# Seven products in another order, and three sums of tokens made later: attention, mixture of experts and a gated layer on one core

## The chip, the cores and the metric

The kernel runs on one core of a Trainium2 chip. The metric is the time of one execution on the device in microseconds (us); the median of several runs counts. Less is better.

## The reference

Three layers follow each other; all inputs of the kernel are 64-bit floats, and the result is a 32-bit float.

```python
attn = softmax(causal(q @ k.T / 8)) @ v            # 4 x 12 heads, 448 tokens, 64 wide
x = attn as [1792, 768]
x = moe(x)      # 8 experts, each takes its 224 best tokens: relu(x @ w1[e]) @ w2[e]
gate = 1 / (1 + exp(-(x @ w_gate)))                # [768, 1536]
val = x @ w_val                                    # [768, 1536]
out = (gate * val) @ w_out                         # [1536, 768]
```

The change touches the last layer alone.

## The kernel before, in words

Attention runs first, then the routing of the tokens, then the eight experts one after the other, and then the gated layer in two halves of 896 tokens: `moe2a` and `moe2b`. A half consists of two blocks of 448 tokens, `bb` = 0 and 1. The hidden width of 1536 is cut into 12 slices `f` of 128. For two slices at a time, both halves make gate and value, multiply them to h, and add h times w_out to `acc` (`out_stage`: 84 matmuls of 384 columns for seven token tiles; it takes h of the even slice first, then h of the odd slice, for each tile). A 32-bit product is made of three matmuls: every operand is split into a high part (a copy by ScalarE, "hi") and the rest (a subtraction, "lo"), and hi·hi, hi·lo and lo·hi are added in PSUM. `h_parts` (lines 933 and 934) does this for h, on ScalarE and then VectorE.

**Weights.** The first half converts the 64-bit weights as they are first used (`conv_split`, lines 83 to 94): ScalarE makes the low word's share (line 83) and a square (line 85), VectorE works through lines 87, 88, 89 and 92, ScalarE makes hi (line 93) and VectorE lo (line 94). Each slice comes as two half tiles. The converted weights are also written to DRAM (`wsc`).

**The first half, `moe2a`**, makes plain products: 72 matmuls of 448 columns for each slice.

**The second half, `moe2b`**, treats two slices times two halves of the width of 768 times two token blocks as a 2 x 2 block product and makes it with seven products of sums in place of eight. The sums of weights are made on GpSimd in `combine`, a pair of slices ahead of their use. The sums of tokens are made once, also on GpSimd: three in `stage` (lines 974 to 976, after four loads of x on SyncE's queue, line 972), one in `stage_parts` (line 984); `stage` is called in `moe2a` ahead of slice 6. The results of the seven products are added up by VectorE (lines 1013 and 1022 to 1026); `done(o, add, e, bb)` finishes h of slice e (0 or 1 of the pair) and block bb: line 1013 the last sum, then for the gate (n = 0) a sigmoid on ScalarE, and for the value (n = 1) line 1019 the product with the gate, and `h_parts`. Then `out_stage` begins with tiles 4, 5 and 6, which need block 1 alone, and goes on to tile 3 and to block 0.

**What sets the order.** TensorE takes its matmuls in the order in which the code writes them. For the other engines and the DMA queues a scheduler picks an order when the kernel is built, from its own estimate and from priorities (`tc.high_priority`); on the chip each engine then works through its fixed list and waits at the first instruction that isn't ready.

Of the kernel before, what the change touches and what calls it, by code (L numbers as in the profile page):

```python
# [7 lines left out]
F32 = mybir.dt.float32  # L8
# [5 lines left out]
OP = mybir.AluOpType  # L14
# [10 lines left out]
HMIN = 3.4332275390625e-05  # L25
# [5 lines left out]
def body(ctx: ExitStack, tc: tile.TileContext, q, k, v, moe_w_gate, moe_w1, moe_w2,  # L31
         w_gate2, w_val2, w_out2, out):
    nc = tc.nc
# [11 lines left out]
    x2_d = dram.tile([2, 128, KD, 448], F32, name="x2_d")  # L45
# [8 lines left out]
    NF = F2 // 128  # L54
# [6 lines left out]
    g64, v64, o64 = (w.bitcast(U32) for w in (w_gate2, w_val2, w_out2))  # L61
    cv = ctx.enter_context(tc.tile_pool(name="cv", bufs=2))

    xst = []

    def conv_half(kind, f, n, hn, ln):
        cs = cv.tile([128, HC, 2], U32, name="cs", bufs=2)
# [11 lines left out]
    def conv_split(cs, hn, ln):  # L79


        hw, lw = cs[:, :, 1], cs[:, :, 0]
        nc.scalar.activation(lw, lw, AF.Copy, scale=2.0 ** -29)
        sq = cv.tile([128, HC], F32, name="sq", bufs=1)
        nc.scalar.activation(sq, hw.bitcast(F32), AF.Square)
        a = cv.tile([128, HC], U32, name="ca")
        nc.vector.tensor_scalar(a, hw, 3, 0x3FFFFFF8, op0=OP.logical_shift_left, op1=OP.bitwise_and)
        nc.vector.scalar_tensor_tensor(a, hw, 0xC0000000, a, op0=OP.bitwise_and, op1=OP.bitwise_or)
        nc.vector.tensor_tensor(a, a, lw, op=OP.add)  # L89

        w_ = a.bitcast(F32)
        nc.vector.scalar_tensor_tensor(w_, sq, HMIN * HMIN, w_, op0=OP.is_ge, op1=OP.mult)  # L92
        nc.scalar.activation(hn, w_, AF.Copy)
        nc.vector.tensor_tensor(ln, w_, hn.bitcast(F32), op=OP.subtract)  # L94
        return w_
# [58 lines left out]
    V = nc.vector  # L154
# [319 lines left out]
    HO = 5000  # L474
# [201 lines left out]
    def wt(dt=F32R):  # L676
        return mp.tile([128, CH], dt, name="w", bufs=WB)
# [53 lines left out]
    def combine(n, f):  # L731
        raw = cv.tile([128, HC, 2], U32, name="cs", bufs=2).rearrange("p f t -> p (f t)").bitcast(F32)
        for e in range(2):
            nc.sync.dma_start(raw[:, e * 768:(e + 1) * 768], wsc[wsc_n["gv", f + e]][:, 0, n * 768:(n + 1) * 768])
        a11, a12, a21, a22 = (raw[:, i * 384:(i + 1) * 384] for i in range(4))
        tl = [(wt(), wt()) for _ in range(2)]
        got = {}

        def parts(m, src, t, s_):
            hi, lo = (x[:, s_ * 384:(s_ + 1) * 384] for x in tl[t])  # L740
            nc.scalar.activation(hi, src, AF.Copy)  # L741
            nc.gpsimd.tensor_tensor(lo, src, hi.bitcast(F32), op=OP.subtract)  # L742
            got[m] = (hi, lo)

        TT = nc.gpsimd.tensor_tensor
        parts(1, a11, 0, 0)
        parts(4, a22, 0, 1)
        TT(a22, a21, a22, op=OP.add)
        parts(5, a22, 0, 2)
        TT(a21, a11, a21, op=OP.subtract)  # L750
        TT(a11, a22, a11, op=OP.subtract)
        parts(6, a11, 0, 3)
        TT(a22, a12, a11, op=OP.subtract)
        parts(7, a21, 1, 0)
        parts(3, a22, 1, 1)
        parts(2, a12, 1, 2)
        return got

    def load_half(kind, a, c, n, raw):
# [12 lines left out]
    def use(key):  # L772
        while key not in W:
            load_chunk()
        return W[key]
# [123 lines left out]
    def xq():  # L899
        return mp.tile([128, 3, 448], F32R, name="xq", bufs=8)  # L900
# [31 lines left out]
    def h_parts(hx, bb, o):  # L932
        nc.scalar.activation(hx[:, 0, bb], o, AF.Copy)
        nc.vector.tensor_tensor(hx[:, 1, bb], o, hx[:, 0, bb].bitcast(F32), op=OP.subtract)  # L934

    def moe2a():
        idxf = m2.tile([128, NT], I32, name="idxf", bufs=1)
        acc = m2.tile([128, NT, DM], F32, name="acc", bufs=1)
        gs = []
        for f in range(NF):  # L940
            if f == NF // 2:
                stage()
            wh, wl = use(("gv", 0, f))
            wv = [(wh[:, n * 768 + d * 128:n * 768 + (d + 1) * 128], wl[:, n * 768 + d * 128:n * 768 + (d + 1) * 128])
                  for n in range(2) for d in range(KD)]
            hx = mp.tile([128, 2, 2, 448], F32R, name="hx", bufs=3)
            for bb in range(2):
                x2h, x2l = X2[bb]
                xx = [(x2h[d // 3][:, d % 3, :], x2l[d // 3][:, d % 3, :]) for d in range(KD)]
                pg = ps.tile([128, 512], F32, name="g", bufs=7)  # L950
                prods(pg[:, :448], list(zip(wv[:KD], xx)))
                gv = m2.tile([128, 448], F32, name="gv", bufs=2)
                nc.scalar.activation(gv, pg[:, :448], AF.Sigmoid)
                pv = ps.tile([128, 512], F32, name="g", bufs=7)
                prods(pv[:, :448], list(zip(wv[KD:], xx)))
                nc.vector.tensor_tensor(pv[:, :448], pv[:, :448], gv, op=OP.mult)
                h_parts(hx, bb, pv[:, :448])
            gs.append(hx)
            if f % 2 == 1:
                out_stage(0, f - 1, gs, acc, idxf, range(NT))  # L960
                gs = []
# [4 lines left out]
    def xs(dt=F32R):  # L966
        return m2.tile([128, 3, 448], dt, name="xs", bufs=6)

    def stage():
        b11, t2, t1, t3, b22, b21 = (xs(F32) for _ in range(6))  # L970
        for t, kh, bb in ((b11, 0, 0), (t3, 0, 1), (b22, 1, 1), (b21, 1, 0)):
            nc.sync.dma_start(t, x2_d[bb][:, 3 * kh:3 * kh + 3])
        TT = nc.gpsimd.tensor_tensor
        TT(t1, t3, b11, op=OP.subtract)
        TT(t2, b22, t1, op=OP.subtract)
        TT(t3, b22, t3, op=OP.subtract)
        XR.update({1: b11, 6: t2, 5: t1, 7: t3, 3: b22, 2: b21})
# [3 lines left out]
    def stage_parts():  # L981
        t4 = cv.tile([128, HC, 2], U32, name="cs", bufs=2).rearrange("p f t -> p (f t)").bitcast(F32)
        XR[4] = t4[:, :3 * 448].rearrange("p (c t) -> p c t", c=3)
        nc.gpsimd.tensor_tensor(XR[4], XR[2], XR[6], op=OP.subtract)
        for m in (1, 6, 5, 7, 3, 2, 4):
            hi, lo = xq() if m == 1 else xs(), xq()
            nc.scalar.activation(hi, XR[m], AF.Copy)
            nc.vector.tensor_tensor(lo, XR[m], hi.bitcast(F32), op=OP.subtract)
            XS[m] = (hi, lo)

    def moe2b():
        idxf = m2.tile([128, NT], I32, name="idxf", bufs=1)
        acc = m2.tile([128, NT, DM], F32, name="acc", bufs=1)
        stage_parts()
        m1, u2, u3 = (cv.tile([128, HC], dt, name=nm, bufs=b).bitcast(F32)[:, :448]
                      for dt, nm, b in ((U32, "ca", 2), (U32, "ca", 2), (F32, "sq", 1)))
        of = o1.rearrange("p t c -> p (t c)").bitcast(F32)
        sgs = [m2.tile([128, 448], F32, name="gv", bufs=2) for _ in range(2)] + [of[:, :448], of[:, 448:]]
        for f in range(0, NF, 2):
            hx = [mp.tile([128, 2, 2, 448], F32R, name="hx", bufs=3) for _ in range(2)]  # L1000
            for n in range(2):
                qd = use((f"s{n}", 1, f))

                def prod(m):
                    o = ps.tile([128, 512], F32, name="g", bufs=7)[:, :448]
                    prods(o, [tuple((t[0][sl], t[1][sl]) for t, sl in ((qd[m], (slice(None), slice(d * 128, (d + 1) * 128))),
                                                                      (XS[m], (slice(None), d))))
                              for d in range(3)])
                    return o

                def done(o, add, e, bb):

                    V.tensor_tensor(o, o, add, op=OP.add)
                    sg = sgs[2 * e + bb]
                    if n == 0:
                        nc.scalar.activation(sg, o, AF.Sigmoid)
                    else:
                        with tc.high_priority(HO):
                            V.tensor_tensor(o, o, sg, op=OP.mult)
                            h_parts(hx[e], bb, o)  # L1020

                nc.scalar.activation(m1, prod(1), AF.Copy)
                V.tensor_tensor(u2, prod(6), m1, op=OP.add)
                p5 = prod(5)
                V.tensor_tensor(u3, prod(7), u2, op=OP.add)
                V.tensor_tensor(u2, p5, u2, op=OP.add)
                done(p5, u3, 1, 1)
                done(prod(3), u2, 0, 1)
                done(prod(2), m1, 0, 0)
                done(prod(4), u3, 1, 0)  # L1030
            out_stage(1, f, hx, acc, idxf, (4, 5, 6, 3, 0, 1, 2))

    ctx.enter_context(tc.manual_schedule(engines={mybir.EngineType.PE}))
# [40 lines left out]
```

## Time and profile before

| | |
|---|---|
| median of 3 runs | 1130.82 us (1128.95 to 1131.06) |
| the profiled execution | 1130.21 us |
| its span, first to last instruction | 1128.4 us |
| TensorE, matmuls | 1076.9 us busy (95%) |
| VectorE | 699.1 us (62%) |
| ScalarE | 439.5 us (39%) |
| GpSimd | 270.2 us (24%) |
| mean granted clock of TensorE | 0.979 |

In the span, attention reaches to about 245 us, the routing to 283, the experts to 602, the first half of the gated layer to 875 and the second half to the end. TensorE is busy nearly throughout, so what counts is where it stands still. The lines below are of three kinds: a line of the waits says who waited for whom, for how long in total, how often, and how long at most; a line of the timeline gives start, duration, engine, line of the code, operation, tile written and tiles read, and in brackets the idle time ahead of it with what ended it; a line of the windows gives a stretch and its length, the busy time of PE (TensorE), its weight loads, DVE (VectorE), ACT (ScalarE) and POOL (GpSimd), then the granted clock, the share of the DMA engines and their rate.

### The profile page before, as it was taken

To read this page: it belongs to the slowest core of one execution; us is meant where nothing else is said; L and a number is where in the kernel's file an instruction comes from. 1 tells how busy PE (TensorE), PEld (TensorE's weight loads), DVE (VectorE), ACT (ScalarE), POOL (GpSimd) and SP (SyncE) were. 2 spreads that over 40 slices of the span, in tenths; PEclk is the share of its full clock that TensorE was granted. 3 is DMA by queue.
4 is the path that set the end of the run, shared out by engine and by line. 5 is a ranking of instruction groups with operands and counts; after the bars stand their busy time and mean duration, and the time that the engine had idled before them with its cause. 6 is when DMAs were issued, how large, how long until landed. Compare 5 with 4: busy or idle time off the path is not lost.

```text
span 1128.4 us, 19849 instructions
## 1 busy us (share of the span) xinstructions
PE 1076.9 (95%) x7401; PEld 1020.8 (90%) x7401; DVE 699.1 (62%) x1980; ACT 439.5 (39%) x846; POOL 270.2 (24%) x371
## 2 busy tenths in 40 slices
PE   6999999982999999999999899999999999999997
PEld 6999999971899999999999799999999899899897
DVE  5777777766555556442557989878736515435535
ACT  4767677730111111123454465543414442322310
POOL 7333333300000000000000300000125746546522
PEclk9999999995999999999999899999999999999999
DMA  8556565525687667786747676655311521220212
GB/s 173 121 124 170 117 166 122 145 82 97 228 197 193 128 178 193 165 210 181 226 154 226 240 250 229 236 169 191 93 81 56 183 87 54 97 99 29 85 57 98
DMA packets 156991, 167.26 MB, mean 148 GB/s; under 512 B 74576, under 2 KB 140128, under 8 KB 156640
## 3 DMA queue, kind: packets, MB, share of 16 engines
q1 hardware_dynamic: 153472, 154.74, 46.1%
q0 software_dynamic: 2496, 11.04, 5.3%
q8 instruction: 58, 0.95, 0.4%
q10 hardware_dynamic: 928, 0.23, 0.1%
q14 instruction: 37, 0.30, 0.1%
HBM read 122.32 MB, written 32.64 MB: 137 GB/s over the span
## 4 chain that ended last, share of the span: by engine, by line
PE 90%; DVE 5%; issue 1%; DMA 1%; POOL 1%; ACT 1%; POOLq 0%; SPq 0%; ACTq 0%; DVEq 0%
PE g L778 67%; PE o L348 8%; PE w L328 4%; PE s L295 3%; PE s L296 2%; PE r L503 2%; PE w L257 1%; PE g L820 1%; DMA x_d<-x2f 1%; PE w L386 1%; PE w L369 1%; DVE ca L89 1%; DVE w L94 1%; DVE ca L92 0%; DVE hx L934 0%
## 5 line engine op out<-in xcount | busy, mean ns | idle before, releaser
L778 PE MATMUL g<-xq,w 128*128 128x448 f32 x1188 | 282.1, 367 | 0.0
L778 PEld LDWEIGHTS g<-xq,w 128*128 128x128 f32 x1188 | 222.7, 188 | 21.4
L778 PE MATMUL g<-w,hx 128*128 128x384 f32 x1008 | 181.6, 338 | 7.9 <-DVE hx L934 5.8
L778 PEld LDWEIGHTS g<-w,hx 128*128 128x128 f32 x1008 | 176.4, 190 | 12.0 <-DVE hx L934 8.3
L778 PE MATMUL g<-xx,w 128*128 128x224 f32 x768 | 151.4, 339 | 0.0
L778 PE MATMUL g<-hx,w 128*128 128x224 f32 x864 | 151.2, 331 | 0.0
L778 PEld LDWEIGHTS g<-hx,w 128*128 128x128 f32 x864 | 137.6, 191 | 2.5 <-issue 1.0
L778 PEld LDWEIGHTS g<-xx,w 128*128 128x128 f32 x768 | 134.9, 191 | 2.2 <-issue 0.2
L778 PE MATMUL g<-xs,w 128*128 128x448 f32 x432 | 124.7, 365 | 0.0
L742 POOL TENSOR_TENSOR w<-cs,w 128x384 fp32r<-128x384 f32 x84 | 84.2, 1024 | 121.4 <-ACT w L741 121.3
L348 PE MATMUL o<-vt,pt 112*112 112x65 f32 x960 | 106.3, 258 | 0.0
L348 PEld LDWEIGHTS o<-vt,pt 112*112 112x112 f32 x960 | 101.9, 178 | 0.0
L923 DVE TENSOR_TENSOR acc<-g,acc 128x384 f32<-128x384 f32 x140 | 75.3, 554 | 33.3 <-PE g L778 32.3
L298 DVE CUSTOM_DVE_ANT_0 sm<-s,mask 112x112 f32<-112x112 f32 (+1 forms) x192 | 78.4, 445 | 23.0 <-PE s L296 23.0
L306 ACT ACTIVATE sm<-sm,mn 112x112 f32<-112x112 f32 (+1 forms) x192 | 90.3, 522 | 5.1 <-DVE mn L298 5.1
L778 PEld LDWEIGHTS g<-xs,w 128*128 128x128 f32 x432 | 81.1, 188 | 6.2
L803 POOL DMA_INDIRECT xg<-x_d,ids x16 | 15.4, 962 | 296.3 <-DVE ids L622 105.4
L268 POOL CAST st<-hi 64x448 fp32r<-64x448 f32 x96 | 53.3, 556 | 133.4 <-ACT hi L263 122.8
L741 ACT ACTIVATE w<-cs 128x384 fp32r<-128x384 f32 x84 | 40.0, 518 | 92.4 <-PE g L778 48.7
L295 PE MATMUL s<-st,st 128*112 128x112 f32 (+1 forms) x192 | 62.2, 339 | 3.0 <-POOL st L268 2.6
L328 PE MATMUL w<-ident,sm 112*112 112x112 f32 x480 | 62.7, 261 | 0.1
L296 PE MATMUL s<-lo,qz 128*112 128x112 f32 (+1 forms) x192 | 56.5, 309 | 0.0
(214 smaller groups left out, 1450.0 us busy)
## 6 DMA issues: line engine op xcount, KB each, us to landing
w<-in_moe_w_dram SPq DMA_DIRECT2D x96, 384.0 KB, 6.6
raw<-in_moe_w_dram SPq DMA_DIRECT2D x32, 384.0 KB, 4.6
cs<-in_moe_w_gate_dram SPq DMA_DIRECT2D x12, 768.0 KB, 4.2
cs<-in_moe_w_val_dram SPq DMA_DIRECT2D x12, 768.0 KB
wsc<-ca SPq DMA_DIRECT2D x24, 384.0 KB, 4.7
cs<-in_moe_w_out_dram SPq DMA_DIRECT2D x12, 768.0 KB, 4.2
wsc<-w SPq DMA_DIRECT2D x12, 768.0 KB, 4.0
cs<-wsc SPq DMA_DIRECT2D x24, 384.0 KB, 3.1
```

Of the source, the lines that this page charges most:

```text
L268: nc.gpsimd.tensor_copy(st[r, h], hi[r].bitcast(F32))
L295: nc.tensor.matmul(ss[j], qq[:, j, qs], kh[:, j, :w], start=True, stop=False)
L296: nc.tensor.matmul(ss[j], QZ[u % NZ][:, j, qs], kl[:, :w], start=False, stop=True)
L298: nc.vector.tensor_tensor_reduce(sm[:, j, :w], ss[j], mask[:, S - w:], op0=OP.add, op1=OP.min, scale=1.0, scalar=3.0e38, accum_out=mn[:, j ...
L306: nc.scalar.activation(sm[:, j, :w], sm[:, j, :w], AF.Exp, bias=mn[:, j:j + 1], scale=-1.0)
L328: nc.tensor.transpose(w[:P, n, :], sm[:, j, c * P:(c + 1) * P], ident[:P, :P])
L348: nc.tensor.matmul(o[:, n, j, :], pt[:, j * (i + 1) + c, :], vt[:, j, c, :], start=c == 0, stop=c == i)
L503: nc.tensor.matmul(c[:, :J], oha[:, tt_, :], cmps[2 * tt_ // T][:, tt_ % (T // 2), :J], start=tt_ == 0, stop=tt_ == T - 1)
L741: nc.scalar.activation(hi, src, AF.Copy)
L742: nc.gpsimd.tensor_tensor(lo, src, hi.bitcast(F32), op=OP.subtract)
L778: nc.tensor.matmul(o, a, b, start=first, stop=last_)
L923: nc.vector.tensor_tensor(ac, po[:, :384], ac, op=OP.add)
```

## The change

Four edits, all in the gated layer:

- `moe2b` makes its seven products in the order 1, 2, 6, 5, 3, 7, 4; before, it was 1, 6, 5, 7, 3, 2, 4. h of slice 0, block 0 is finished first, then slice 0, block 1, then slice 1, block 1 (which needs products 7 and 5), then slice 1, block 0.
- `combine` makes the sums of weights in an order to fit, and places the parts of products 1, 2, 5, 6 in its first tile and 3, 7, 4 in its second. The number of copies, subtractions and sums stays.
- `stage` is called ahead of the products of slice 11 in place of slice 6, and its four loads wait for line 92 of the last half tile of slice 11's weights.
- `h_parts` in `moe2a` gets a high priority.

```diff
-    xst = []
+    xst, cvi = [], []
...
-        nc.vector.scalar_tensor_tensor(w_, sq, HMIN * HMIN, w_, op0=OP.is_ge, op1=OP.mult)
+        cvi.append(nc.vector.scalar_tensor_tensor(w_, sq, HMIN * HMIN, w_, op0=OP.is_ge, op1=OP.mult).ins)
...
...
         parts(1, a11, 0, 0)
-        parts(4, a22, 0, 1)
-        TT(a22, a21, a22, op=OP.add)
-        parts(5, a22, 0, 2)
-        TT(a21, a11, a21, op=OP.subtract)
-        TT(a11, a22, a11, op=OP.subtract)
-        parts(6, a11, 0, 3)
-        TT(a22, a12, a11, op=OP.subtract)
-        parts(7, a21, 1, 0)
-        parts(3, a22, 1, 1)
-        parts(2, a12, 1, 2)
+        parts(2, a12, 0, 1)
+        TT(a11, a11, a21, op=OP.subtract)
+        TT(a21, a21, a22, op=OP.add)
+        parts(5, a21, 0, 2)
+        TT(a21, a22, a11, op=OP.subtract)
+        parts(6, a21, 0, 3)
+        TT(a12, a12, a21, op=OP.subtract)
+        parts(3, a12, 1, 0)
+        parts(7, a11, 1, 1)
+        parts(4, a22, 1, 2)
...
         for f in range(NF):
-            if f == NF // 2:
+            wh, wl = use(("gv", 0, f))
+            if f == NF - 1:
                 stage()
-            wh, wl = use(("gv", 0, f))
...
-                h_parts(hx, bb, pv[:, :448])
+                with tc.high_priority(HO):
+                    h_parts(hx, bb, pv[:, :448])
...
         for t, kh, bb in ((b11, 0, 0), (t3, 0, 1), (b22, 1, 1), (b21, 1, 0)):
-            nc.sync.dma_start(t, x2_d[bb][:, 3 * kh:3 * kh + 3])
+            d_ = nc.sync.dma_start(t, x2_d[bb][:, 3 * kh:3 * kh + 3])
+            tc.add_manual_dep(d_.ins, cvi[-1].name, mybir.DependencyInfo(mybir.DependencyClass.Sync,
+                                                                         mybir.DependencyReason.DATA),
+                              reason="the weights first")
...
                 nc.scalar.activation(m1, prod(1), AF.Copy)
+                done(prod(2), m1, 0, 0)
                 V.tensor_tensor(u2, prod(6), m1, op=OP.add)
                 p5 = prod(5)
-                V.tensor_tensor(u3, prod(7), u2, op=OP.add)
-                V.tensor_tensor(u2, p5, u2, op=OP.add)
-                done(p5, u3, 1, 1)
-                done(prod(3), u2, 0, 1)
-                done(prod(2), m1, 0, 0)
-                done(prod(4), u3, 1, 0)
+                V.tensor_tensor(u3, p5, u2, op=OP.add)
+                done(prod(3), u3, 0, 1)
+                V.tensor_tensor(u2, prod(7), u2, op=OP.add)
+                done(p5, u2, 1, 1)
+                done(prod(4), u2, 1, 0)
```

SyncE's queue in the first pairs of `moe2a`: `x_d` is the array of tokens in DRAM, `cs` a half tile of 64-bit weights, `wsc` the converted weights in DRAM.

```order
 L719 DMA wsc<-ca 128x768
 L74 DMA cs<-in_moe_w_gate_dram 128x6x256
-L972 DMA xs<-x_d 128x1344 x4
 L74 DMA cs<-in_moe_w_val_dram 128x6x256
 L724 DMA wsc<-w 128x1536
```

The four loads of tokens leave this place. They come again near the end of `moe2a`, behind the write of slice 11's last half tile:

```order
 L77 DMA cs<-in_moe_w_out_dram 128x1536
 L719 DMA wsc<-ca 128x768
+L973 DMA xs<-x_d 128x1344 x4
 L734 DMA cs<-wsc 128x768 x2
 L724 DMA wsc<-w 128x1536
```

The last load of w_out's weights stands ahead of them, and the first loads for `combine` behind them.

VectorE's list at the end of the value's seven products, before the change: `g_10577` is the bank of product 5, `g_10603` of 3, `g_10617` of 2, `g_10631` of 4; `hx_10421` is h of slice 0, `hx_10422` of slice 1; L1013 is the last sum, L1019 the product with the gate, L934 makes lo of h.

```order
L1013 TENSOR_TENSOR g_10577<-g_10577,sq_10418 128x448
L1013 TENSOR_TENSOR g_10603<-g_10603,ca_10417 128x448
L1019 TENSOR_TENSOR g_10577<-g_10577,o1_80 128x448
L1019 TENSOR_TENSOR g_10603<-g_10603,gv_10420 128x448
L1013 TENSOR_TENSOR g_10617<-g_10617,ca_10416 128x448
L934 TENSOR_TENSOR hx_10422<-g_10577,hx_10422 128x448
L1019 TENSOR_TENSOR g_10617<-g_10617,gv_10419 128x448
L1013 TENSOR_TENSOR g_10631<-g_10631,sq_10418 128x448
L934 TENSOR_TENSOR hx_10421<-g_10603,hx_10421 128x448
L1019 TENSOR_TENSOR g_10631<-g_10631,o1_80 128x448
L934 TENSOR_TENSOR hx_10421<-g_10617,hx_10421 128x448
L934 TENSOR_TENSOR hx_10422<-g_10631,hx_10422 128x448
```

Behind the last sum of product 4 stood lo of slice 0, block 1. The same place after the change, where `g_10602` is product 3, `g_10616` is 7, `g_10591` is 5 and `g_10631` is 4 (L1017 is now the last sum, L1023 the product with the gate, L1032 the sum with product 7):

```order
L1017 TENSOR_TENSOR g_10602<-g_10602,sq_10418 128x448
L1023 TENSOR_TENSOR g_10602<-g_10602,gv_10420 128x448
L1032 TENSOR_TENSOR ca_10417<-g_10616,ca_10417 128x448
L934 TENSOR_TENSOR hx_10421<-g_10602,hx_10421 128x448
L1017 TENSOR_TENSOR g_10591<-g_10591,ca_10417 128x448
L1017 TENSOR_TENSOR g_10631<-g_10631,ca_10417 128x448
L1023 TENSOR_TENSOR g_10591<-g_10591,o1_80 128x448
L1023 TENSOR_TENSOR g_10631<-g_10631,o1_80 128x448
L934 TENSOR_TENSOR hx_10422<-g_10591,hx_10422 128x448
L934 TENSOR_TENSOR hx_10422<-g_10631,hx_10422 128x448
```

Behind the last sum of product 4 stand now the product with the gate, and both lo, of slice 1, block 1.

## Rows read from the trace of the kernel before

**Rows 1.** Waits of PE, in the span from 600 us.

```profile
PE g L778 <- DVE hx L934: 5.8, 6, 1.9
```

**Rows 2.** Timeline of PE where the first half begins.

```profile
632.15 0.69 PE L778 MATMUL g<-w,hx 128*128 128x384 f32 x3
634.84 1.01 PE L778 MATMUL g<-w,hx 128*128 128x384 f32 x2 [2.00 <-ACT hx L933]
637.70 15.80 PE L778 MATMUL g<-w,hx 128*128 128x384 f32 x79 [1.85 <-DVE hx L934]
653.33 27.02 PE L778 MATMUL g<-xq,w 128*128 128x448 f32 x130
```

**Rows 3.** Timeline of SP, POOL and DVE ahead of it.

```profile
613.53 1.96 SPq L972 DMA_DIRECT2D xs<-x_d  x4
618.37 0.38 SPq L74 DMA_DIRECT2D cs<-in_moe_w_val_dram  x1
620.15 3.32 POOL L974 TENSOR_TENSOR xs<-xs 128x1344 f32<-128x1344 f32 x1 [5.04 <-DMA xs<-x_d]
620.96 3.33 DVE L94 TENSOR_TENSOR w<-ca,w 128x768 fp32r<-128x768 f32 x1
623.55 3.68 POOL L975 TENSOR_TENSOR xs<-xs 128x1344 f32<-128x1344 f32 x1
627.19 3.80 POOL L976 TENSOR_TENSOR xs<-xs 128x1344 f32<-128x1344 f32 x1
627.96 0.61 DVE L934 TENSOR_TENSOR hx<-g,hx 128x448 fp32r<-128x448 f32 x1
628.50 3.30 DVE L92 SCALAR_TENSOR_TENSOR ca<-sq,ca 128x768 f32<-128x768 f32 x1
```

**Rows 4.** Windows of one microsecond: after this wait, and at one in the second half.

```profile
635.00:636.00 1.00, 0.84 (x2) 0.34 (x2) 0.66 (x1) 0.22 (x1) 0.00 (x0) 0.50 0.00 0
901.00:902.00 1.00, 0.21 (x2) 0.06 (x1) 1.00 (x3) 0.89 (x3) 1.00 (x2) 1.00 0.00 0
```

**Rows 5.** Page, part 6: issues, KB of each, microseconds from issue to landing.

```profile
cs<-in_moe_w_gate_dram SPq DMA_DIRECT2D x12, 768.0 KB, 4.2
```

**Rows 6.** Timeline of SP, DVE, POOL and PE around slice 9's products.

```profile
797.43 0.32 SPq L719 DMA_DIRECT2D wsc<-ca  x1
804.74 1.83 DVE L94 TENSOR_TENSOR w<-ca,w 128x768 fp32r<-128x768 f32 x2 [2.67 <-ACT w L93]
807.96 1.82 DVE L88 SCALAR_TENSOR_TENSOR ca<-cs,ca 128x768 uint32<-128x768 uint32 x2
809.69 1.82 DVE L89 CUSTOM_DVE_ANT_0 ca<-cs,ca 128x1536 uint16<-128x1536 uint16 x2
810.87 3.60 POOL L984 TENSOR_TENSOR cs<-xs 128x1344 f32<-128x1344 f32 x1 [179.88 <-DVE ca L89]
811.97 3.32 DVE L92 SCALAR_TENSOR_TENSOR ca<-sq,ca 128x768 f32<-128x768 f32 x1
815.21 0.61 DVE L934 TENSOR_TENSOR hx<-g,hx 128x448 fp32r<-128x448 f32 x1
816.05 14.73 PE L778 MATMUL g<-w,hx 128*128 128x384 f32 x84
```

**Rows 7.** Timeline at the end of the second half's first pair of slices.

```profile
900.54 0.61 PE L778 MATMUL g<-w,hx 128*128 128x384 f32 x2
900.73 0.63 DVE L1013 TENSOR_TENSOR g<-g,sq 128x448 f32<-128x448 f32 x1
901.27 0.62 DVE L934 TENSOR_TENSOR hx<-g,hx 128x448 fp32r<-128x448 f32 x1
901.80 0.62 DVE L1019 TENSOR_TENSOR g<-g,o 128x448 f32<-128x448 f32 x1
901.94 2.35 PE L778 MATMUL g<-w,hx 128*128 128x384 f32 x12 [0.79 <-DVE hx L934]
902.46 0.55 ACT L933 ACTIVATE hx<-g 128x448 fp32r<-128x448 f32 x1 [0.57 <-DVE g L1019]
```

More of the change, by code (lines that the diff above doesn't have):

```diff
@@ L969, in stage @@
     def stage():
-        b11, t2, t1, t3, b22, b21 = (xs(F32) for _ in range(6))
+        b11, b21, t2, t1, b22, t3 = (xs(F32) for _ in range(6))
         for t, kh, bb in ((b11, 0, 0), (t3, 0, 1), (b22, 1, 1), (b21, 1, 0)):
-            nc.sync.dma_start(t, x2_d[bb][:, 3 * kh:3 * kh + 3])
+            d_ = nc.sync.dma_start(t, x2_d[bb][:, 3 * kh:3 * kh + 3])
+            tc.add_manual_dep(d_.ins, cvi[-1].name, mybir.DependencyInfo(mybir.DependencyClass.Sync,
+                                                                         mybir.DependencyReason.DATA),
+                              reason="the weights first")
         TT = nc.gpsimd.tensor_tensor
@@ L984, in stage_parts @@
         nc.gpsimd.tensor_tensor(XR[4], XR[2], XR[6], op=OP.subtract)
-        for m in (1, 6, 5, 7, 3, 2, 4):
+        for m in (1, 2, 6, 5, 3, 7, 4):
             hi, lo = xq() if m == 1 else xs(), xq()
```

## The prediction

> **What bounds the kernel now.** I read the shares of busy time first: TensorE is busy for 95% of the span, no other engine for more than 62%. So only a place where TensorE stands still or runs slowly can give or take time. The waits of TensorE come next, from 600 us on [rows 1]: 5.8 us in six waits on the lo part of h. The only other line of that view is one wait of 2.00 us on its hi part [rows 2]; none is on weights or on sums of tokens. The timeline puts them in two kinds of places.
>
> The first is the start of `moe2a`. At 632.15 us TensorE begins the first `out_stage`, does three matmuls, waits for hi until 634.84, does two more, and waits for lo until 637.70 [rows 2]. The next products begin at 653.33, so these 84 matmuls took 21.18 us; an undisturbed set takes 14.73 us [rows 6]. This place costs 6.45 us. Part of that is no wait: the granted clock stands at 0.50 (1.2 GHz) in the microsecond from 635 [rows 4], after the first of the two waits. The 79 matmuls behind 637.70 took 15.63 us where 79 x 14.73 / 84 = 13.85 us would do: 1.8 us for the clock.
>
> Why h came late is seen one step earlier [rows 3]. SyncE issues the four loads of tokens at 613.53, and at 620.15 GpSimd begins the three sums (lines 974 to 976), which run back to back until 630.99. In that stretch three of VectorE's conversions, one beside each sum (the first and the last are shown), take 3.3 us and more, where undisturbed ones take about 0.9 (1.83 us for two in [rows 6]), while line 934, which reads h from PSUM, keeps its 0.61. From 620.96 to 631.80 VectorE got through three conversions and one line 934: 10.84 us for what else takes 3 x 0.87 + 0.53 = 3.14 (starts of successive instructions in [rows 6] and [rows 7] lie so far apart). The sums cost VectorE 7.7 us.
>
> A rule of the Trainium skill bears on this (SBUF — State Buffer, section "Who interferes with whom"): a VectorE instruction with two SBUF inputs contends with a GpSimd instruction that reads SBUF, the pair of ports is locked for a whole instruction, and whoever issues first gets it. The trace agrees on the lock; on who gets it, it shows turns: the sums themselves grow from 3.32 to 3.68 and 3.80 us [rows 3]. By the rule alone, sums that issue second would wait, VectorE would lose nothing at their new place, and the time would be that of the first rival below; by the trace's turns it is that of the forecast.
>
> The second kind is the end of each pair of slices in `moe2b`. At 900.54 TensorE starts `out_stage`, and its third matmul (lo of slice 0, block 1) waits until 901.94, because line 934 for it stands behind the last sum of product 4 on VectorE, at 901.27 [rows 7]. Two matmuls take 0.35 us, so 1.05 us are lost. Of the 5.8 us, 1.85 belong to the first place; the other five waits are 0.79 us each, one in each of the first five pairs.
>
> **Part by part.** *The stall at 632 goes: -6.45 us.* No sums and no loads of tokens stand there any more. TensorE needs lo of slice 1, block 0 at 632.15 + 5 x 0.175 = 633.0. What is late next is the load of value weights, issued at 618.37 [rows 3] since it waits for a half tile that VectorE reads until then; it lands 4.2 us later [rows 5], at 622.6, and VectorE's list now has four of that half tile's conversions, three of the gate's and line 956 ahead of this lo. At 0.87 and 0.53 us each, with two more short ones, these end at about 631.4 in place of 637.6: a margin of 1.6 us. Ends: -6.45 (all gone) to -3 (half of it stays, if that load lands 4 us later still).
>
> *The sums at their new place: +8.4 us.* The loads are now issued behind line 719 at 797.43 [rows 6]. All of this stretch moves with TensorE (the conversions wait for tiles that TensorE frees), so I use the times of before for it. From issue to the first sum 6.6 us passed [rows 3]; so the sums begin at about 804.4, and run until about 815. That is where VectorE converts slice 11's and w_out's last half tiles without a gap: from 804.74 lines 94, 87, 88, 89 and 92 follow each other, all SBUF to SBUF like those that were held up, up to line 934 at 815.21, which makes lo of slice 9, block 0 [rows 6]. TensorE wants that at 816.05 + 5 x 0.175 = 816.9, and it is done at 815.8: a margin of 1.1 us, with one held-up instruction (811.97, by line 984) already in it. Three more cost 7.7 us, so TensorE loses 6.6. As at 632, it waits for hi, does two matmuls and waits for lo, both waits longer than there; I add the 1.8 us of the slow clock. Ends: 0 (GpSimd gives way, or the sums fit into VectorE's idle time ahead of 804.74, 2.67 us of it in [rows 6], and behind the h parts) and 9.5 (the 7.7 us and the clock's 1.8, with no margin). I take 8.4 since the rows of the same three sums against the same lines are nearest. SyncE's loads that now stand behind the waiting ones (line 734, for `combine`) and GpSimd's line 984 have time: TensorE first uses these sums of weights and tokens at about 875.
>
> *The new order of the products: +5.4 us.* In `moe2b` product 4 is still last. Now slice 1, block 1 is the late one, since it needs products 7 and 5, and VectorE's list has, behind the last sum of product 4: product with the gate for slice 1, block 1; the same for block 0; lo; lo. I lay it on the clock of [rows 7]. The last sum starts at 900.73; the product with the gate takes line 934's place at 901.27; ScalarE's hi follows 0.66 later (901.80 to 902.46 in the rows), 901.93 to 902.48; lo then takes until 903.15, and TensorE starts 0.05 behind it, at 903.2. It needs this lo for its sixth matmul (slice 0's three come first, and their h is ready early), at 900.54 + 5 x 0.175 = 901.42. It loses 1.77 us in place of 1.05. The sixth pair, which showed no wait, runs by the same list, so 6 x 1.77 - 5 x 1.05 = 5.4 us. Ends: 0 (some earlier finish on VectorE makes up for it) and 16 (should 1.77 us of waiting also drop the clock, 6 x 1.8 more; at 0.79 us of waiting it stays at 1.00, after 2.00 us it fell [rows 4]).
>
> *The rest: 0.* The order in `combine` changes no count (7 copies, 7 subtractions and 4 sums in both) and frees tiles earlier; no wait of TensorE in [rows 1] is for weights, so nothing can be won, and sums that come a product late still lie ahead of use. The priority in `moe2a` moves line 934 ahead of conversions; its gain is inside the first term. Each at -0.5 to 0.5.
>
> **Sum.** -6.45 + 8.4 + 5.4 = +7.35. The profiled execution took 1130.21 us, 0.6 below the median of the runs shown, and inside their spread of 2.1, so I set nothing against that: 1130.21 + 7.35 = 1137.6 us.
>
> **Rivals.** *The sums are hidden at the new place.* For it: VectorE has 2.67 us idle just ahead, and loads that land at another time than I assume meet fewer conversions. Against it: the list from 804.74 on is tight, and three sums are 10 us long. Time: 1130.21 - 6.45 + 5.4 = 1129.2; with a third of the loss, 1132. That is no change.
>
> *The change does all it can: faster.* Sums hidden, and at the ends of the pairs slice 1's h comes as early as slice 0's did, because ScalarE has no copy of weights ahead of it or VectorE starts product 4's sum later than the other instructions; the waits stay at 1.05 us or go. Time: 1130.21 - 6.45 = 1123.8, at best 1118.5. The price at the pairs decides: below 4.2 us for all six, with the sums hidden, it is faster. Against it stands VectorE's list, in which slice 1's product with the gate follows product 4's sum.
>
> *The clock drops at every pair.* Two waits close together, 1.4 us for hi and then a short one for lo, cost the half clock as at 635. Time: 1137.6 + 6 x 1.8 = 1148.4. Against it: 1.77 us is less than the 4 us of waiting at 632.
>
> *The first stall stays,* from the late load of value weights, so that the change doesn't do what it says: 1137.6 + 6.45 = 1144.
>
> **Chances.** Forecast 0.55; sums hidden 0.22; faster 0.1; clock 0.07; first stall stays 0.06. A difference of 0.2% (2.3 us) is about what can be told from none here. Faster by more: 0.12, the third case and a little of the second. Within: 0.2. Slower: 0.68. The likeliest case's own range, from its ends, is 1133 to 1141; with the hidden sums below and the first stall above, 1128.5 to 1143.
>
> **What would show it.** Right: no wait of TensorE on h at the first `out_stage`, and clock 1.00 there; three sums of about 3.5 us on GpSimd near 800 us and three conversions on VectorE held up to 3.3 us or more beside them; a wait of TensorE of several microseconds at slice 8's `out_stage` with the clock at 0.50 after it; and in `moe2b` six waits, first on line 933, then on line 934, some 1.8 us lost in each. Wrong: conversions of 0.95 us beside the sums, or a set of 84 matmuls at slice 8 in 14.7 us, would end the second term; waits in `moe2b` not above 0.8 us the third.

## The result, and the profile after

The changed kernel takes 1144.92 us (median of 6 runs, 1142.4 to 1149.31) against 1131.18 for the one before (6 runs, 1128.95 to 1132.03): the medians lie 13.7 us apart, and the ratio is 1.0127, 95% interval 1.0103 to 1.0151, so 1.3% slower. The forecast was 1137.6, slower, with a range up to 1143.0: the sign was right and the size was not. Its profiled execution took 1142.4 us with a span of 1140.5, 12.1 above the span of before, and these 12.1 can be placed.

The waits of TensorE from 600 us, which answer to [rows 1]:

```profile
PE g L778 <- ACT hx L933: 14.4, 9, 5.2
PE g L778 <- DVE hx L934: 4.2, 5, 2.1
```

In place of 7.8 us of waits there are 18.6: those on hi (line 933) grew from 2.0 to 14.4, those on lo (line 934) fell from 5.8 to 4.2. The timeline of TensorE at the first half's first two `out_stage`s answers to [rows 2]:

```profile
631.00 0.69 PE L778 MATMUL g<-w,hx 128*128 128x384 f32 x3
632.53 0.62 PE L778 MATMUL g<-w,hx 128*128 128x384 f32 x2 [0.85 <-ACT hx L933]
633.72 6.54 PE L778 MATMUL g<-w,hx 128*128 128x384 f32 x36 [0.57 <-DVE hx L934]
640.47 7.72 PE L778 MATMUL g<-w,hx 128*128 128x384 f32 x43 [0.21 <-DVE hx L934]
648.03 29.91 PE L778 MATMUL g<-xq,w 128*128 128x448 f32 x144
677.78 0.69 PE L778 MATMUL g<-w,hx 128*128 128x384 f32 x3
679.02 0.62 PE L778 MATMUL g<-w,hx 128*128 128x384 f32 x2 [0.54 <-ACT hx L933]
680.30 6.51 PE L778 MATMUL g<-w,hx 128*128 128x384 f32 x36 [0.66 <-DVE hx L934]
687.42 7.74 PE L778 MATMUL g<-w,hx 128*128 128x384 f32 x43 [0.61 <-DVE hx L934]
695.00 10.28 PE L778 MATMUL g<-xq,w 128*128 128x448 f32 x49
```

The first set of 84 matmuls takes 648.03 - 631.00 = 17.03 us: 4.15 less than the 21.18 of before, not 6.45 less. And the second set (slices 2 and 3), which before ran from 683.09 to 697.65 without a wait, now takes 695.00 - 677.78 = 17.22, which is 2.66 more. Together the start gives 1.49 us.

What stands ahead of h is seen in the timeline of SyncE, ScalarE and VectorE, the answer to [rows 3]:

```profile
621.69 0.38 SPq L74 DMA_DIRECT2D cs<-in_moe_w_gate_dram  x1
627.11 0.63 DVE L956 TENSOR_TENSOR g<-g,gv 128x448 f32<-128x448 f32 x1
629.64 0.91 ACT L83 ACTIVATE cs<-cs 128x768 uint32<-128x768 uint32 x1 [4.45 <-DMA cs<-in_moe_w_gate_dram]
630.71 0.56 DVE L87 TENSOR_SCALAR ca<-cs 128x768 uint32<-128x768 uint32 x1 [2.97 <-DMA wsc<-ca]
631.97 0.52 ACT L933 ACTIVATE hx<-g 128x448 fp32r<-128x448 f32 x1
633.05 0.62 DVE L934 TENSOR_TENSOR hx<-g,hx 128x448 fp32r<-128x448 f32 x1
```

h of slice 1, block 0 could be taken from 627.74 on, when line 956 is done. But ScalarE's list has line 83 ahead of it, the first step of a conversion whose weights, issued at 621.69, are there only 7.95 us later; VectorE's list has line 87 ahead of it, which waits 2.97 us until a store has freed its `ca` buffer. Nothing holds up a conversion here any more; h queues behind two instructions that wait for transfers. At the second set it is the same: line 87 waits 2.57 us for a store at 673.58, and line 956 stands behind it.

At the sums' new place the timeline of SyncE, GpSimd, VectorE and TensorE answers to [rows 6]:

```profile
797.37 2.50 SPq L973 DMA_DIRECT2D xs<-x_d  x4
805.39 3.08 POOL L978 TENSOR_TENSOR xs<-xs 128x1344 f32<-128x1344 f32 x1 [191.43 <-DMA xs<-x_d]
805.42 3.46 DVE L87 TENSOR_SCALAR ca<-cs 128x768 uint32<-128x768 uint32 x1
808.55 3.27 POOL L979 TENSOR_TENSOR xs<-xs 128x1344 f32<-128x1344 f32 x1
808.81 7.56 DVE L88 SCALAR_TENSOR_TENSOR ca<-cs,ca 128x768 uint32<-128x768 uint32 x2
811.78 3.76 POOL L980 TENSOR_TENSOR xs<-xs 128x1344 f32<-128x1344 f32 x1
819.27 1.01 PE L778 MATMUL g<-w,hx 128*128 128x384 f32 x2 [5.16 <-ACT hx L933]
821.72 0.61 DVE L934 TENSOR_TENSOR hx<-g,hx 128x448 fp32r<-128x448 f32 x1
822.39 15.36 PE L778 MATMUL g<-w,hx 128*128 128x384 f32 x79 [2.11 <-DVE hx L934]
837.59 2.63 PE L778 MATMUL g<-xq,w 128*128 128x448 f32 x12
```

Three conversions beside three sums take 11.0 us in place of 2.4 (0.55 and the 1.82 for two of [rows 6]). Lo of slice 9, block 0 comes at 821.72, and TensorE, which entered slice 8's `out_stage` at 813.42, leaves it at 837.59: 24.17 us in place of 14.56. Of these 9.61 us, 8.1 are the delay of the sixth matmul (822.39 - 813.42, less five of 0.175) and 1.5 are lost by the 79 behind it. The windows that answer to [rows 4], the first of them in this stall, the second at an end of a pair:

```profile
820.00:821.00 1.00, 0.28 (x1) 0.00 (x0) 1.00 (x1) 0.00 (x0) 0.98 (x1) 0.50 0.00 0
909.00:910.00 1.00, 0.50 (x2) 0.30 (x2) 0.92 (x2) 0.98 (x2) 1.00 (x2) 1.00 1.00 378
```

The granted clock is 0.50 (1.2 GHz) behind the 5.16 us wait and 1.00 at the pair. That pair is the answer to [rows 7], timeline of TensorE, its weight loads (PEld), VectorE and ScalarE:

```profile
906.95 1.39 DVE L1017 TENSOR_TENSOR g<-g,ca 128x448 f32<-128x448 f32 x2
907.51 0.68 PE L778 MATMUL g<-w,hx 128*128 128x384 f32 x3
908.25 1.15 DVE L1023 TENSOR_TENSOR g<-g,o 128x448 f32<-128x448 f32 x2
908.90 1.08 ACT L933 ACTIVATE hx<-g 128x448 fp32r<-128x448 f32 x2 [0.47 <-DVE g L1023]
909.48 1.16 DVE L934 TENSOR_TENSOR hx<-g,hx 128x448 fp32r<-128x448 f32 x2
909.50 2.17 PE L778 MATMUL g<-w,hx 128*128 128x384 f32 x9 [1.31 <-ACT hx L933]
910.16 1.37 PEld L778 LDWEIGHTS g<-w,hx 128*128 128x128 f32 x8 [0.36 <-DVE hx L934]
```

Hi follows the product with the gate, which follows both last sums (line 1017), as the list had it. TensorE waits 1.31 us for hi; lo then holds up the weight load of the sixth matmul by 0.36, which the waits of TensorE's matmuls don't list. That load starts at 910.16, 1.78 us behind 907.51 + 5 x 0.175; both waits come in each of the six pairs. `moe2b` takes 258.59 us from 881.91 to the end, where it took 253.47: 5.12 more.

Sum: start of `moe2a` 0.59 earlier and its first 144 matmuls 0.56 shorter, -1.15; first two `out_stage`s -4.15 + 2.66; slice 8 +9.61; `moe2b` +5.12: 12.09. The -1.15 can't be put down to the change: it touches no stage ahead of `moe2a`, and `p_products` and `p_prio` below, which leave the sums in place, also take 29.20 us for these first 144 matmuls. The other terms come to 13.24.

### The profile page after: what moved, and what is told of

It reads as the page before. It is cut to its first block, busy times and chain, and to the rows that moved or that the text cites. A ratio compares the mean times of both kernels' runs of the same rounds, so it can differ in the third digit from the quotient of the medians.

```text
span 1140.5 us, 19872 instructions
## 1 busy us (share of the span) xinstructions
PE 1078.3 (95%) x7401; PEld 1020.1 (89%) x7401; DVE 700.7 (61%) x1980; ACT 439.4 (39%) x846; POOL 270.1 (24%) x371
## 4 chain that ended last, share of the span: by engine, by line
PE 72%; DVE 12%; DMA 10%; issue 2%; ACT 2%; POOL 2%; POOLq 0%; SPq 0%; DVEq 0%; ACTq 0%
PE g L778 49%; PE o L348 8%; PE w L328 4%; DMA wsc<-ca 3%; PE s L295 2%; PE s L296 2%; DMA cs<-in_moe_w_gate_dram 2%; DVE ca L88 2%; DMA xg<-x_d,ids 2%; DVE ca L89 2%; DMA cs<-in_moe_w_out_dram 2%; DVE acc L923 2%; DVE ca L92 1%; PE w L257 1%; PE r L503 1%
## 5 line engine op out<-in xcount | busy, mean ns | idle before, releaser
L778 PE MATMUL g<-w,hx 128*128 128x384 f32 x1008 | 184.0, 339 | 18.8 <-ACT hx L933 14.4
```

Of the source, the lines that this page charges most:

```text
L778: nc.tensor.matmul(o, a, b, start=first, stop=last_)
```

## The experiments

The table gives the times, with the ratio to before as timed beside each kernel (medians 1130.57 to 1132.05), and two lengths from each profile: from the first product of `moe2a` to the first matmul on `xs` (the first half), and from there to the end of the span. They leave out the stages ahead, whose length differs by up to 4.7 us between these profiles.

| kernel | median us | ratio to before, 95% | first half | second |
|---|---|---|---|---|
| before | 1131.18 | | 274.40 | 251.61 |
| the change | 1144.92 | 1.0127 [1.0103, 1.0151] | 281.96 | 256.74 |
| p_products | 1135.53 | 1.0051 [1.0034, 1.0068] | 272.24 | 256.71 |
| p_sums | 1139.07 | 1.0078 [1.0059, 1.0097] | 282.13 | 251.69 |
| p_prio | 1131.13 | 1.0006 [0.9994, 1.0017] | 274.38 | 251.64 |
| b_behind_wo | 1129.59 | 0.9989 [0.9977, 1.0001] | 271.58 | 251.59 |
| a_behind_wo | 1134.70 | 1.0045 [1.0032, 1.0058] | 272.05 | 256.81 |
| b_loads_early | 1124.41 | 0.9952 [0.9939, 0.9965] | 268.05 | 251.74 |
| b_wo_hfirst | 1149.46 | 1.0159 [1.0145, 1.0174] | 287.59 | 256.01 |
| b_best | 1145.03 | 1.0139 [1.0123, 1.0156] | 287.73 | 251.50 |
| c_order | 1125.83 | 0.9945 [0.9932, 0.9958] | 267.92 | 251.64 |
| c_loads_old | 1127.73 | 0.9958 [0.9945, 0.9971] | 268.07 | 251.72 |
| c_after_loads | 1130.00 | 0.9981 [0.9970, 0.9992] | 267.23 | 256.77 |
| c_best | 1121.26 | 0.9908 [0.9894, 0.9922] | 267.24 | 248.02 |

**The parts alone.** `p_products` has the edits in `combine`, `stage_parts` and `moe2b`; `p_sums` those in `conv_split`, `moe2a` and the loads of `stage`; `p_prio` the priority.

> The kernel before with the new order of the seven products and the sums of weights to fit; the sums of tokens stay where they were. Theory (VectorE's list puts slice 1's product with the gate behind product 4's sum): about 5 us slower than before, 1136 us, with six waits of TensorE on line 933 of about 1.3 us each and a period of the pairs of 42.1 us in place of 41.3; the stall at the first out_stage stays at about 6.5 us. Rival (this order costs nothing by itself): the same time as before.

> The kernel before with the three sums of tokens moved behind slice 11's weights as in the change, and nothing else. Theory (the sums take VectorE's port wherever conversions run): 8 to 9 us slower, about 1139.5 us: some 9.4 us lost at slice 8's out_stage, and only 1 to 3 us won at the start, since the weights come late there anyway. Rival (the loss comes from the products' order and the priority): within 2 us of before.

> The kernel before with a high priority for h_parts in moe2a, and nothing else. Theory: within 1 us of before, since the sums still hold VectorE up ahead of the first out_stage. Rival (the priority puts h ahead of conversions, which then come late at slice 2's out_stage): 2 to 3 us slower, with a second stall there.

The ratios less one, 0.51%, 0.78% and 0.06%, add up to 1.35%; the whole change costs 1.27%. So within the intervals the parts add up, and the priority is worth nothing. `p_products` has the six waits of 1.3 us on hi; its first `out_stage` takes 19.58 us, where 21 was expected (the last section has the difference). `p_sums` alone shows both what failed and what held: its first two `out_stage`s take 17.00 and 17.21 us, slice 8's 24.40.

**The sums behind everything.** `b_behind_wo` is before with `stage` called behind slice 10's last w_out weights; `a_behind_wo` is the changed kernel with the same edit. In both the four loads wait for line 92 of the last conversion.

```diff
-            if f == NF // 2:
-                stage()
...
             gs.append(hx)
+            if f == NF - 1:
+                use(("wo", 0, f - 1))
+                stage()
```

> The kernel before with the sums of tokens behind the last conversion of all (w_out's last half tile, at about 817 us) in place of slice 11's weights. Theory (lock of the port): VectorE has no SBUF-to-SBUF conversion left then, so slice 8's out_stage takes 14.7 us and nothing is lost there; what the start gives remains, 1 to 5 us: 1126 to 1130 us. Rival (the loads of tokens or the late sums themselves hold TensorE up): a stall of 5 us and more at slice 8 or at the start of moe2b.

> The changed kernel with the sums of tokens behind the last conversion of all in place of slice 11's weights, all else kept. Theory (the parts add up): the 9.4 us at slice 8's out_stage go, and about 5 us of the products' order stay: 1134.5 to 1136 us. Rival (a part of the changed kernel's loss needs both edits): 1138 us and more.

With no conversion left beside the sums, slice 8's `out_stage` takes 14.56 us again (815.17 to 829.73), and the change becomes 10.2 us faster. But in `b_behind_wo` the start still takes 16.33 and 17.17 us: of 6.45 us in the first half, 2.8 come, and its time is not clear of before's.

**Loads early, sums late.** `b_loads_early` issues the four loads of tokens where before has them and keeps the sums behind everything.

```diff
+    def stage_loads():
+        ST.extend(xs(F32) for _ in range(6))
...
-        TT(t1, t3, b11, op=OP.subtract)
+        g_ = TT(t1, t3, b11, op=OP.subtract)
+        tc.add_manual_dep(g_.ins, cvi[-1].name, ...
...
             if f == NF // 2:
-                stage()
+                stage_loads()
...
+            if f == NF - 1:
+                use(("wo", 0, f - 1))
+                stage()
```

> The kernel before with the four loads of tokens at their old place and only the three sums moved behind the last conversion. It asks what made the first stall: the sums or the loads. Theory (the sums hold VectorE's port): the first out_stage loses about 2 us, as in the kernel with both moved, not 6.5, and the time is 1128 to 1130 us. Rival (the loads fill the DMA queues, and the weights behind them come late): 6 us and more are lost there, and the time is that of before, 1131 us or more.

It is the fastest of these, faster than theory and rival had it, and here the forecast's term appears whole: the first `out_stage` takes 14.59 us in place of 21.18. (The first half is 6.35 us shorter: 0.57 are gained ahead of it, and slice 8's set takes 15.37, beside the late sums.) The timeline of its TensorE, ScalarE and VectorE at the place of [rows 2 and 3]:

```profile
625.00 0.63 DVE L956 TENSOR_TENSOR g<-g,gv 128x448 f32<-128x448 f32 x1
627.25 0.55 ACT L933 ACTIVATE hx<-g 128x448 fp32r<-128x448 f32 x1
628.56 0.62 DVE L934 TENSOR_TENSOR hx<-g,hx 128x448 fp32r<-128x448 f32 x1
631.20 14.75 PE L778 MATMUL g<-w,hx 128*128 128x384 f32 x84
631.37 0.92 ACT L83 ACTIVATE cs<-cs 128x768 uint32<-128x768 uint32 x1 [0.45 <-DMA cs<-in_moe_w_gate_dram]
632.43 0.56 DVE L87 TENSOR_SCALAR ca<-cs 128x768 uint32<-128x768 uint32 x1
645.79 29.91 PE L778 MATMUL g<-xq,w 128*128 128x448 f32 x144
```

The weights are no earlier than in the changed kernel (line 83 begins at 631.37, 9.5 us behind the issue at 621.89), but h stands ahead of them in both lists, and TensorE waits for nothing here. From 617 us up to this lo both lists are those of before, and only the sums beside them are gone: lo begins at 628.56 in place of 637.02. So the sums made the first stall. In `p_sums`, `b_behind_wo` and the changed kernel, which issue the loads of tokens late, lines 83 and 87 of the next half tile stand ahead of h. That the loads' place in SyncE's queue leads the scheduler to these other lists can be read from the programs; why it does so stays open.

**All conversions behind h.** `b_wo_hfirst` is `b_behind_wo` with the first ScalarE and the first VectorE instruction of every conversion issued behind h of two slices back; `b_best` has besides, in `moe2b`, the last sum of product 4 behind lo of slice 0, block 1.

```diff
-        nc.scalar.activation(lw, lw, AF.Copy, scale=2.0 ** -29)
+        with tc.issue_after(hp[-4][0]) if len(hp) > 3 else ExitStack():
+            nc.scalar.activation(lw, lw, AF.Copy, scale=2.0 ** -29)
```

> The kernel with the sums of tokens behind the last conversion, and in moe2a each conversion's first instruction on ScalarE and VectorE put behind h of the slice two back, block 0. It asks why 2.3 and 2.6 us are still lost at the first two out_stages. Theory (in ScalarE's and VectorE's lists h stands behind conversions that wait for their weights): both stalls go, 4 to 5 us, 1125 us. Rival (the weights are converted too late as such, since loads, stores and VectorE are full there): h comes early but TensorE then waits for weights, and the time stays within 1.5 us of 1129.5 or gets worse.

> As the last, and in moe2b, with the old order of the products, the last sum of product 4 is put behind lo of slice 0, block 1 on VectorE. It tests the reading of the second half's waits: the list of VectorE alone sets them. Theory: the five waits of 0.79 us fall to 0.1 or less, 3 to 4 us less than the last kernel: 1121 to 1122 us. Rival (ScalarE's copies of weights ahead of hi set them): less than 1 us is won.

`b_wo_hfirst` is 18 us slower than before, where 1125 us was expected. Its second `out_stage` takes 14.57 us, but its first 19.43: h of slice 1, block 0 is on time, and h of block 1 stands behind conversions (waits of 1.20 us for hi and 1.06 for lo). Most of the loss lies elsewhere, since the edit moved everything later. The timeline of its GpSimd and TensorE:

```profile
856.93 3.08 POOL L980 TENSOR_TENSOR xs<-xs 128x1344 f32<-128x1344 f32 x1 [238.26 <-DMA xs<-x_d]
893.69 0.74 PE L780 MATMUL g<-xs,w 128*128 128x448 f32 x1 [15.35 <-ACT w L743]
```

The loads of tokens, which wait for the last conversion, are issued at 849.67, some 35 us later than in `b_behind_wo` (814.78); the sums of tokens and of weights follow, and `moe2b` waits 15.35 us for them. `b_best` against it tells about the pairs: 4.4 us less, all in the second half, where 3 to 4 were expected; the waits at the pairs are gone.

**Only the two lists, only two slices.** `c_order` is `b_behind_wo` with that order for gate and val of slices 3 and 5 alone.

```diff
-        return conv_split(cs, hn, ln)
+        return conv_split(cs, hn, ln, hp[2 * f - 4 + n] if kind == "gv" and f in (3, 5) else None)
...
-        nc.scalar.activation(lw, lw, AF.Copy, scale=2.0 ** -29)
+        with tc.issue_after(h[0]) if h else ExitStack():
+            nc.scalar.activation(lw, lw, AF.Copy, scale=2.0 ** -29)
...
+        with tc.issue_after(h[1]) if h else ExitStack():
```

> b_behind_wo with the lists alone changed: on ScalarE and VectorE the first steps of the conversions of slices 3 and 5 (gate and val halves) are issued behind h of slices 1 and 3, so that h no longer stands behind a conversion that waits for its load and for the store that frees its buffer. Theory (what was left of the first stall is the order of the two lists): the two first w_out products take 14.6 us each instead of 16.3 and 17.2, so 4.4 us less than b_behind_wo: 1125.2 us. Rival (the transfers or the conversions are themselves too late, and something else, such as gate and val of the next slices, waits instead): within 1 us of b_behind_wo, 1129.6.

Measured 1125.83, against the theory's 1125.2. The timeline of its ScalarE, VectorE and TensorE:

```profile
630.71 0.89 ACT L86 ACTIVATE sq<-cs 128x768 f32<-128x768 f32 x1 [1.65 <-DMA cs<-in_moe_w_gate_dram]
631.73 15.43 PE L780 MATMUL g<-w,hx 128*128 128x384 f32 x84
632.07 0.62 DVE L936 TENSOR_TENSOR hx<-g,hx 128x448 fp32r<-128x448 f32 x1 [2.02 <-ACT hx L935]
632.61 0.55 DVE L89 TENSOR_SCALAR ca<-cs 128x768 uint32<-128x768 uint32 x1
676.76 14.73 PE L780 MATMUL g<-w,hx 128*128 128x384 f32 x84
```

Lo now stands ahead of the step that waits for the store, and the first two sets take 15.27 (to 647.00) and 14.57 us. The loads of tokens still come behind w_out's weights, as in `b_behind_wo`, and the weights no earlier: ScalarE waits for the gate's until 630.71, 8.0 us behind their issue at 622.68. So what was left of the two stalls was the order of the lists, not the transfers themselves. The 0.7 us still lost at the first set fit that: hi stands behind line 86, the square of the same weights, which the edit leaves where it was.

**Loads at the old place, sums at the change's.** `c_loads_old` is `b_loads_early` with `stage()` ahead of slice 11's products.

> before with the loads of the token blocks at the old place, and only the three sums on GpSimd moved to where the change puts them (behind slice 11's gate and val weights). Theory: the first stall goes whole (-6.3 us against before) and the one at slice 8 comes (+9.5): 1134 us, 5 us under p_sums (1139.1), whose loads moved too. Rival (it is the waiting loads that make slice 8 late, not the sums): about 1125, the time of b_loads_early.

My theory was wrong here, and the rival nearer: the first half is as long as that of `b_loads_early` (268.07 and 268.05). The timeline of GpSimd and TensorE:

```profile
794.31 3.08 POOL L982 TENSOR_TENSOR xs<-xs 128x1344 f32<-128x1344 f32 x1 [175.39 <-DVE ca L92]
800.50 3.11 POOL L987 TENSOR_TENSOR xs<-xs 128x1344 f32<-128x1344 f32 x1
813.00 1.04 PE L778 MATMUL g<-w,hx 128*128 128x384 f32 x5
814.60 13.97 PE L778 MATMUL g<-w,hx 128*128 128x384 f32 x79 [0.56 <-DVE hx L934]
```

With the tokens already in SBUF the sums begin 11.1 us earlier than in the changed kernel and end at 803.6, in a stretch where VectorE has little to do (2.95 us busy in the 10 from 794). Slice 8's set takes 15.41 us. So the stall there came from the loads' wait: it pushed the sums onto w_out's conversions.

**The order of products on a clean first half; and the best.** `c_after_loads` is the changed kernel with loads early and sums behind everything; `c_best` is `b_loads_early` with the edit in `moe2b` that `b_best` had.

```diff
-                    V.tensor_tensor(o, o, add, op=OP.add)
+                    with tc.issue_after(lo01[0]) if n and (e, bb) == (1, 0) else ExitStack():
+                        V.tensor_tensor(o, o, add, op=OP.add)
```

> The changed kernel with the loads of the token blocks at the old place and the three sums behind slice 10's w_out weights, so that of the change its order of products and its priority are left. Theory (the parts add): b_loads_early (1124.4) plus the order of products (+4.7): 1129.1 us, 1.5 us under before, 5.6 under a_behind_wo. Rival (with other lists the first stall comes back): 1134.7 as a_behind_wo.

> b_loads_early, and in the second half VectorE's last sum of product 4 issued behind lo of slice 0's block 1. Theory: each of the six pairs loses its wait for that lo (3.9 us in five waits, and the part of the step that goes with it): 1124.4 less 4 = 1120.4 us. Rival (the gain of b_best over b_wo_hfirst came from elsewhere, as its first w_out product differed too): 1124.4 as before.

In the second half, `c_after_loads` is 5.0 us above `b_loads_early`, like every kernel with the new order. `c_best` is 3.7 us below it, shows no wait of TensorE from 600 us to the end, and is the best version found: 1121.26 us, 0.9% faster than before and 2.1% (1121.26 / 1144.92) faster than the change. The timeline of its VectorE at the end of the first pair:

```profile
894.52 0.62 DVE L934 TENSOR_TENSOR hx<-g,hx 128x448 fp32r<-128x448 f32 x1
895.06 0.62 DVE L1027 TENSOR_TENSOR g<-g,sq 128x448 f32<-128x448 f32 x1
```

Lo of slice 0, block 1 goes ahead of product 4's last sum; in [rows 7] it stood behind it.

## Why the prediction was right in sign and wrong in size

- **The step that failed: "The stall at 632 goes: -6.45 us".** Measured: -4.15 at this `out_stage`, within its ends (-6.45 to -3), and +2.66 at the second, for which the sum had no term: -1.49 together. The sums were rightly named as the cause of the stall (`b_loads_early` keeps before's lists there without the sums beside them and takes 14.59 us). But I took the lists for given but for the sums, and priced only VectorE's instructions ahead of lo. I left out ScalarE's list, where hi stood behind a conversion whose weights took 7.95 us, and the store that VectorE's conversion waited for; the margin of 1.6 us was used up by these. (The terms given for it, from 622.6 seven at 0.87, line 956 and two short ones at about 0.53, end at about 630.3 and not 631.4, so by its own prices the margin was nearer 2.7.) The value weights, named as late next, were in time: line 83 took them at 621.75. And I looked at one `out_stage`, while the second lost 2.66 us for the same reason. `c_order` shows it by putting the two lists right: 15.27 and 14.57 us.
- **"The sums at their new place: +8.4".** Measured +9.61, just above the upper end of 9.5, by the mechanism foretold: three conversions beside three sums, two waits, clock at 0.50. The delay was 8.1 us where 6.6 were foretold, the clock 1.5 for 1.8. `p_sums` has it alone, `b_behind_wo` takes it away. The rule of the Trainium skill that was weighed (SBUF — State Buffer, "Who interferes with whom") would have let the sums wait had VectorE issued first. The first sum began at 805.39, 0.03 us ahead of line 87, and line 87 waited; from there on the trace shows both sides slowed in turns.
- **"The new order of the products: +5.4".** Measured +5.12 in the change and 5.1 in `p_products`, on hi first and lo behind it as worked out: 1.78 us lost in a pair, 1.77 foretold. The sixth pair of before, taken as losing nothing, lost 0.3 (its third matmul starts at 1107.84, 0.64 behind the first). The clock stayed at 1.00 in the windows read.
- **"The rest: 0".** Right for the priority: `p_prio` 1.0006 [0.9994, 1.0017]. The order in `combine` has no run of its own; no wait of TensorE from 600 us is on weights.
- **The sum.** 7.35 foretold, 12.09 in the spans: the start is off by 4.96, the sums by 1.2, the order by -0.3, and -1.15 came from ahead of the first `out_stage`, not from the change. The medians differ by 1.6 more than the spans; the profiled execution is the shortest of the change's six, and its 13.24 without the -1.15 are close to the 13.7 of the medians.
- **The rivals.** "The first stall stays" (1144, chance 0.06) has the nearest time, by chance and not by its mechanism: most of that stall went, other terms made up for it, and the load named in it, that of value weights, was not the late one. "Sums hidden" is nearly what `c_loads_old` does, once the loads don't wait.

## What to carry to other kernels

A stall that is removed gives back its time only as far as what is next in line on every engine of its chain is on time: go through each in-order list ahead of the late result, ScalarE's as well as VectorE's, with the loads and stores that its instructions wait for, and through the next period too. Work that is moved must be moved with its latency: make the data wait in SBUF and delay only the instruction that disturbs. A dependency that is meant to delay one instruction can also give the scheduler another order far from it, so compare the lists at the places that have no margin, and pin those few, not all.

## What the runs showed of the hardware

Beside GpSimd's sums of 1344 fp32 in SBUF, VectorE's step with a single SBUF input was held up as well as those with two: line 87 took 3.46 us in place of 0.55, two of line 88 took 7.56 in place of 1.82. A sum takes 3.08 us alone (`c_loads_old`) and mostly up to 3.8 in company. But it is not always VectorE that pays. The timeline of GpSimd and VectorE in `p_products`, whose list on VectorE is that of before in this stretch:

```profile
621.38 4.82 POOL L974 TENSOR_TENSOR xs<-xs 128x1344 f32<-128x1344 f32 x1 [5.80 <-DMA xs<-x_d]
621.42 0.95 DVE L94 TENSOR_TENSOR w<-ca,w 128x768 fp32r<-128x768 f32 x1
622.28 0.95 DVE L89 CUSTOM_DVE_ANT_0 ca<-cs,ca 128x1536 uint16<-128x1536 uint16 x1
```

Here the first sum gives way to two conversions, which before took 3.33 and 3.83 us, and the first `out_stage` takes 19.58 us in place of 21.18. In `p_sums` line 87, 0.02 us behind the first sum, keeps its 0.55, and the sum takes 3.52. What decides it no run here shows.

A half tile of weights took 7.95, 8.0 (`c_order`) and 9.5 us (`b_loads_early`) from issue to use, where the median from issue to landing is 4.2 [rows 5]; the mean busy share of the DMA engines from 624 to 631 us was 0.98, 0.95 and 1.04.
